# The second chunk's C product as seven block products, in a gated mix of a state-space layer and a dense layer

## The chip, the cores and the metric

The kernel runs on one core of a Trainium2 chip. The metric is the device time of one execution in microseconds, given as the median of the runs.

## What is computed

The input x has 2048 tokens of 640 features. Two branches are computed from it and mixed by a gate for each token:

```python
g = sigmoid((x * gate_w).sum(-1, keepdims=True))
h[t] = Lam_bar * h[t-1] + B_bar @ x[t]            # complex, 640 states
a = 2.0 * einsum("blp,dp->bld", h, Cmat).real + x * Dskip
b = gelu(x @ w1 + b1) @ w2 + b2                   # 640 -> 1728 -> 640
return g * a + (1 - g) * b
```

Data are bfloat16; the output is bfloat16.

## The kernel before, in words

**Tiling.** The tokens are cut into four chunks of 512 (CH). A chunk has four token tiles of 128; the first two are its first half, the last two its second. The 640 states are five rows of 128 (KS), the 640 output features two halves of 320 (HD).

**Stages of a chunk c.** `ff1(c)` multiplies x by w1 (65 + 20 matmuls), and ScalarE writes the gelu into `gel[c]`. `ssm(c)` multiplies x by B (50 matmuls): for each of the five rows ScalarE evicts two PSUM banks into a `bu` tile (eight of them, in turn). VectorE then works on the row (`scan_ops`): three products and sums turn it (`cos_in`, `sin_in`, `sum_in`, which frees `bu`), two scans along the tokens, three more turn it back (`cos_out`, `sin_out`, `sum_out`) into the state tile `hs[c]`. Rows are counted through all chunks: chunk 0 has rows 0 to 4, chunk 3 rows 15 to 19. `fin_b(c)` multiplies `gel[c]` by w2 and leaves (1-g)·b in float32 tiles `gbs`. Then the states are multiplied by C and combined with `gbs` into the output tile `ot`, which a DMA stores.

**Two forms of the C product.** `hs[c]` has four blocks of 128 x 5 x 256: a and b are the real and imaginary states of the chunk's first half, g21 and d those of the second half. C has four blocks as well: C11 and C12 are the two halves of `CT_re` by output feature, C21 and C22 those of `CT_im`.
- `fin_a(c)` (line 799) multiplies directly: 4 token tiles x 2 halves x 10 matmuls = 80 (line 812). The skip term x·D is put into the PSUM banks beforehand by ScalarE (`seed`, line 664, which also loads the x tile of the chunk after), and one VectorE instruction for each half of a tile makes the output (line 817). Chunks 0 and 1 use it.
- `fin_s(c)` (line 865) is a Strassen form in Winograd's ordering: seven block products instead of eight, 7 x 2 x 5 = 70 matmuls (line 877). It needs sums of blocks. From the states: M7 = a - g21, then g21 + d in g21's place, M6 = a - (g21 + d), M3 = b + M6 (`h_sums`, line 838, four VectorE instructions of 128x1280). From C: U7 = C12 - C22, U6 = U7 - C11, and U5 and U4, which are C22 and C21 plus U6. Partial sums X are forked by ScalarE into other banks (Y, Z, W), product 7 is added on VectorE (`part_7`, line 901), the skip term is added to `gbs` by VectorE (`skip_in`, line 855), and `done` (line 886) makes the output. Products run in the order 1, 7, 2, 6, 5, 3, 4, each for two token tiles. Chunks 2 and 3 use it. `fin_b` is of the same form.

**Sums made by transfers.** `plus(dst, src)` (line 676) is a DMA issued by POOL that adds src onto dst in SBUF; `minus(dst, src)` (line 681) is a ScalarE copy with scale -1. `minus_c(c)` and `minus_d(c)` make the sums that `fin_b(c)` needs, in the tiles N3 and N2, from `gel[c]`. U4 to U7 are made in this way during `ff1(3)`, out of two copies on SP, two negations on ScalarE and four additions.

**Order.** The order of instructions on each engine is that of the program (a manual schedule). For VectorE a small planner keeps clocks for TensorE, ScalarE and VectorE. The operations of scan rows wait in a list `pend`. `dve_now(ready, cost, fn)` first lets out of the list what would start, by VectorE's clock, ahead of `ready`, and then emits fn. `let_out(0, c)` lets out everything up to the last row of chunk c:

```python
def let_out(until, chunk=-1):
    while pend:
        ready, cost, fn, _ = pend[0]
        start = max(ck.dve, ready)
        if start >= until and not any(x[3] == chunk for x in pend if chunk >= 0):
            return
        pend.pop(0); fn(); ck.dve = start + cost
```

SP and POOL work through their transfers in program order too; a transfer that waits holds those behind it. TensorE's order around the change is ff1(2), fin_a(0), ssm(2), fin_b(1), fin_a(1), ssm(3), ff1(3), fin_b(2), fin_s(2), fin_b(3), fin_s(3).

**Names that the change touches.** `xA` and `xB` hold transposed x: chunks 0 and 3 in xA, 1 and 2 in xB. `load_xT(3)` (line 128) is issued ahead of ssm(2). `gates(c)` (line 644) makes columns of g and 1-g. `skips(c, a)` multiplies x tiles by D on VectorE. `gated(c)` (line 849) puts g·x·D of two token tiles into the tiles GS[c] on ScalarE. `settle` issues small ScalarE work for the scans' carries. The dictionaries given to a stage hold work to be issued at numbered places of it ("hooks").

Of the kernel before, what the change touches and what calls it, by code (L numbers as in the profile page):

```python
# [16 lines left out]
P = 128  # L17
# [25 lines left out]
def kernel(  # L43
# [40 lines left out]
    xA, xB = (const.tile([P, KD, CH], BF16, name=n) for n in ("xA", "xB"))  # L84
    xT = [xA, xB, xB, xA]
    w1a_sb = const.tile([P, KD, cut1], BF16, name="w1a_sb")
# [10 lines left out]
    CT_re = const.tile([P, KS, D], BF16, name="CT_re")  # L97
    CT_im = const.tile([P, KS, D], BF16, name="CT_im")
    TCOS = const.tile([P, KS, CH], BF16, name="TCOS")
    TSIN2 = const.tile([P, KS, 2, CH], BF16, name="TSIN2")  # L100
# [75 lines left out]
    HC = CH // 6 + 1  # L176
    tfi = work.tile([P, HC], I32, name="e", bufs=1)
    nc.gpsimd.iota(tfi[:], pattern=[[1, HC]], base=0, channel_multiplier=0)
    rows(nc.gpsimd, prmA[0:KS, :], A_log_dt)
# [6 lines left out]
    NP = NQ + HC  # L186
    tf = const.tile([P, NP], F32, name="tf")
    for i, m in enumerate((1.0, float(CH), float(CH // 2), float(2 * HC - 2))):
# [70 lines left out]
    nc.vector.memset(halfpi[:], HALF_PI)  # L259
    nc.vector.tensor_copy(out=tf[:, NQ:NP], in_=tfi[:])  # L260
    ones = lambda n: nc.const_aps.tensor(1.0, [P, n], BF16)
# [103 lines left out]

    scr = gelp.tile([P, KF * CH // 2], F32, name="gel")
    gel_tile(0)
# [19 lines left out]
    cq = col("cq", n=NQ * KS)  # L387
    kk = work.tile([P, KS, NP], I32, name="bu", bufs=8)
    sth, cth = sq[:, 0:KS], cq[:, 0:KS]
# [25 lines left out]
    nc.vector.tensor_tensor(out=thp_c[:], in0=dt16[:], in1=limp[:], op=ALU.mult)  # L415
    nc.vector.tensor_tensor(out=u, in0=tf[:].rearrange("p (o i) -> p o i", o=1).to_broadcast([P, KS, NP]), in1=over(thp_c[:], NP), op=ALU.mult)
    part(0, 2)
# [58 lines left out]
    def inputs(c, ks):  # L476
        bu = work.tile([P, 2, CH], BF16, name="bu", bufs=8)
        for ri, BT in enumerate((BT_re, BT_im)):
            p = bank()
            for kd in range(KD):  # L480
                nc.tensor.matmul(p[:], lhsT=BT[ks >= KSA][:, kd, (ks % KSA if ks < KSA else ks - KSA) * P:][:, 0:P], rhs=xT[c][:, kd, :],  # L481
                                 start=(kd == 0), stop=(kd == KD - 1))
                pe(CH)
            nc.scalar.activation(out=bu[:, ri, :], in_=p[:], func=ACT.Identity)  # L484
            act(0.6)
        return bu, ck.act
# [64 lines left out]
    def scan_ops(c, ks, bu, ready):  # L551
# [55 lines left out]
        def sum_out():  # L607
# [3 lines left out]

        new = [(ready, 0.61, cos_in, -1), (0, 0.61, sin_in, -1), (0, 0.61, sum_in, -1), (0, 1.23, lambda: scan(0), -1),
               (0, 1.21, lambda: scan(1), -1), (0, 0.3 if c == 0 else 0.1 if c < NCH - 1 else 0, ends if c < NCH - 1 else lambda: None, -1),
               (0, 0.61, cos_out, -1), (0, 0.61, sin_out, -1), (0, 0.63, sum_out, c)]
        old = latest.ops
# [28 lines left out]
    def gates(c):  # L644
        sl = slice(c * TPC, (c + 1) * TPC)

        def f():
            nc.vector.tensor_scalar(out=gcol[:, 0, sl], in0=gz[:, sl], scalar1=0.5, scalar2=0.5, op0=ALU.mult, op1=ALU.add)
            nc.vector.tensor_scalar(out=gcol[:, 1, sl], in0=gz[:, sl], scalar1=-0.5, scalar2=0.5, op0=ALU.mult, op1=ALU.add)
            nc.vector.tensor_scalar(out=gcol[:, 2, sl], in0=gz[:, sl], scalar1=0.5, scalar2=-0.5, op0=ALU.mult, op1=ALU.add)  # L650

        dve_now(ck.act + 0.3 if c > 0 else ck.pe, 0.2, f)
# [8 lines left out]
    def skip(ti):  # L661
        dve_now(ck.pe, 0.45, lambda: nc.vector.tensor_tensor(out=xn[ti][:], in0=xn[ti][:], in1=Dbc[:], op=ALU.mult))

# [57 lines left out]
    def fin_b(c, at={}, gs=None):  # L721
# [58 lines left out]
        both("X", N2, TB)  # L780
        fork("X", "Z")
        if c < NCH - 1:
            part_7()
# [45 lines left out]
    narrow = lambda t, n: t.rearrange("p k t -> p (k t)")[:, 0:n]  # L829
    U5, U7, U6, U4 = (narrow(t, KS * HD).rearrange("p (k d) -> p k d", k=KS) for t in (BT_re[1][:], BT_im[1][:], xB[:], w1b_sb[:]))  # L830
    M6, M7 = (t[:].rearrange("p k t -> p (k t)").rearrange("p (k t) -> p k t", k=KS) for t in (BT_im[0], BT_re[0]))
    M3 = narrow(xA[:], KS * HT).rearrange("p (k t) -> p k t", k=KS)
    C11, C12, C21, C22 = (t[:, :, h * HD:(h + 1) * HD] for t in (CT_re, CT_im) for h in range(2))

    def add(out, x, y, op):
        return lambda: nc.vector.tensor_tensor(out=flat(out), in0=flat(x), in1=flat(y), op=op)

    def h_sums(c):
        (a, b), (g21, d) = ([hs[c][:, i, r] for r in range(2)] for i in range(2))
        steps = []  # L840
        for out, x, y, op in ((M7, a, g21, ALU.subtract), (g21, g21, d, ALU.add), (M6, a, g21, ALU.subtract), (M3, b, M6, ALU.add)):
            steps.append(lambda fn=add(out, x, y, op): dve_now(0, 0.8, fn))
        return steps, (a, M7, M6, b, g21, M3, d), (C11, U7, U6, C21, U5, C22, U4)

    wide = [narrow(w1a_sb[:], 6 * D)[:, j * 2 * D:(j + 1) * 2 * D].bitcast(F32) for j in range(3)]
    wide += [xA[:].rearrange("p k t -> p (k t)")[:, KS * HT:].bitcast(F32), narrow(w1c_lo[:], 2 * D).bitcast(F32)]
    GS = {2: wide[0:2], 3: wide[3:5]}
# [7 lines left out]
    def skip_in(c, tiles, d0, d1, ready=0):  # L855
        for a in tiles:
            ti = c * TPC + a
            if a >= H:
                dve_now(ready, 0.82, lambda: nc.vector.tensor_tensor(out=gbs[ti][:], in0=gbs[ti][:], in1=GS[c][a - H], op=ALU.add))
                continue  # L860
            dve_now(ready, 0.88 if d1 - d0 > HD else 0.48, lambda: nc.vector.scalar_tensor_tensor(
                out=gbs[ti][:, d0:d1], in0=xn[ti][:, d0:d1], scalar=gcol[:, 0, ti:ti + 1],
                in1=gbs[ti][:, d0:d1], op0=ALU.mult, op1=ALU.add))

    def fin_s(c, lhs, rhs, at={}):
        A = dict(zip((1, 7, 6, 2, 5, 3, 4), lhs))
# [19 lines left out]
        def done(t, j, half, h, d0=0, d1=HD):  # L886
            ti = c * TPC + half * H + j
            first = ti not in ots
            if first:
                ots[ti] = fwork.tile([P, D], BF16, name="ot", bufs=4)  # L890
            o = h * HD
            dve_now(ck.pe + 0.2, 0.54, lambda: nc.vector.scalar_tensor_tensor(  # L892
                out=ots[ti][:, o + d0:o + d1], in0=t[j][:, d0:d1], scalar=gcol[:, 0, ti:ti + 1],
# [7 lines left out]
        def part_7(j):  # L901
            gb, ti = gbs[c * TPC + H + j], c * TPC + H + j
            wide = lambda t: t.rearrange("p (h d) -> p h d", h=2)
            dve_now(ck.act, 0.88, lambda: nc.vector.scalar_tensor_tensor(
                out=wide(gb[:]), in0=q[j][:].rearrange("p (o d) -> p o d", o=1).to_broadcast([P, 2, HD]),
                scalar=gcol[:, 3, ti:ti + 1], in1=wide(gb[:]), op0=ALU.mult, op1=ALU.add))
# [10 lines left out]
        for j in range(H):  # L917
            product(Q, 7, j, True)
            q[j] = fwork.tile([P, HD], F32, name="gq", bufs=2)
            nc.scalar.activation(out=q[j][:], in_=Q[j][:, 0:HD], func=ACT.Identity)  # L920
            act(0.44)
# [48 lines left out]
    def sums(c):  # L970
# [16 lines left out]
    gates(2)  # L987
    fin_a(0, sums(1))
    load_xT(3)
    ssm(2, {KS - 1: lambda: skips(1)})  # L990
    fin_b(1, seeds(1))
    fin_a(1, {**sums(2), 3: lambda: minus(U6, C22, 1.5)})
    ssm(3)
    gel_tile(3)
    nc.sync.dma_start(out=U7, in_=C12)
    steps, lhs, rhs = h_sums(2)
    ff1(3, 0, {1: lambda: (minus(U5, C11, 1.5), plus(U7, U6), plus(U5, C12), plus(U6, U5)),
               5: lambda: (skips(2), let_out(0, 2), [f() for f in steps[:3]]),
               7: lambda: (skips(2, H), [load_xn((NCH - 1) * TPC + H + j, narrow(w1a_sb[:], 6 * D)[:, (4 + j) * D:(5 + j) * D]) for j in range(H)]),
               10: lambda: (nc.sync.dma_start(out=U4, in_=C21), plus(U4, U6))})  # L1000
    for a, t in ((0, w1c_hi[:].rearrange("p k f -> p (k f)")[:, 0:D]), (1, xB[:].rearrange("p k t -> p (k t)")[:, KS * HD:KS * HD + D])):
        load_xn((NCH - 1) * TPC + a, t)
    gates(3)
    nc.vector.tensor_scalar(out=gcol[:, 3, NT - 2 * TPC:NT], in0=gcol[:, 0, NT - 2 * TPC:NT], scalar1=-1.0, scalar2=None, op0=ALU.mult)
    steps[3]()
    fin_b(2, {1: lambda: (gated(2), skips(3, H)),
              2: lambda: minus_c(3),
              3: lambda: (gated(3), skip_in(2, (0, 1), 0, HD))}, GS[2])
    last, lhs3, _ = h_sums(3)
    fin_s(2, lhs, rhs, {0: lambda: skip_in(2, (0, 1), HD, D, ck.act + 0.5), 1: lambda: (minus_d(3), skips(3))})  # L1010
    fin_b(3, {0: lambda: (let_out(1e9), [f() for f in last]),
              3: lambda: skip_in(3, (0, 1), 0, HD)}, GS[3])
    skip_in(3, (H, H + 1), 0, D)
    skip_in(3, (0, 1), HD, D)
    fin_s(3, lhs3, rhs)

# [29 lines left out]
```

## Time and profile before

| what | value |
|---|---|
| runs (3) | 206.68 to 207.22 us, median 206.85 |
| profiled execution | 206.56 us, its span 204.8 us |
| granted TensorE clock | 1.00 |
| fin_a(1) | 119.19 to 130.06 us, 80 matmuls |
| fin_s(2) | 168.80 to 178.41 us, 70 matmuls |
| VectorE busy in 119.19 to 130.06 | 10.87 us of 10.87 |
| VectorE busy in 168.80 to 178.41 | 7.58 us of 9.61 |
| ScalarE busy in 119.19 to 130.06 | 8.41 us |
| share of DMA time in 105.70 to 119.19 | 0.28 |

How to read the profile: all times count from the span's start. The page gives the busy time of each engine and, in 40 slices of the span, its busy share in tenths. The chain of waits is followed back from the last instruction; each of its rows is a start, a length and an engine with the tile that it writes and the line of the code. Groups and timelines name an instruction as out<-in with the shape, and in brackets the idle time ahead of it and what ended that. PE is TensorE, DVE VectorE, ACT ScalarE, POOL GpSimd and SP SyncE.

### The profile page before, as it was taken

The numbers are of one execution on the slowest core, as the hardware profiler recorded it, in microseconds if no ns is written. First come the engines' busy times: TensorE is split into PE (matmuls) and PEld (weight loads), VectorE is DVE, ScalarE is ACT, GpSimd is POOL, SyncE is SP. The second block draws the span as 40 slices with busy tenths as digits, with TensorE's granted clock in tenths as the row PEclk, the third lists the DMA queues.
The fourth block names the chain that finished last, engine by engine and source line by source line (L and its number), as shares of the span: only waits on it lengthen the run. The fifth ranks groups of instructions, "written<-read, shape, count | busy, mean of one in ns | idle before, by whom it ended". The sixth has DMA issues, their size and how long they took to land.

```text
span 204.8 us, 3592 instructions
## 1 busy us (share of the span) xinstructions
PE 200.6 (98%) x1301; PEld 119.3 (58%) x1301; DVE 186.6 (91%) x314; ACT 140.7 (69%) x271; POOL 50.6 (25%) x83
## 2 busy tenths in 40 slices
PE   8999999999999999999999999999999999999993
PEld 5744544454477544675457777544446777777762
DVE  2799999999999999999999999999999999686573
ACT  4696856997866799991764899266776699255520
POOL 8506930313330410031001052200412170124000
PEclk9999999999999999999999999999999999999999
DMA  6999999999999160159932369912596989719303
GB/s 192 193 144 223 194 303 158 203 224 287 177 210 219 23 109 15 50 104 239 194 90 53 74 120 234 235 35 80 89 190 121 182 159 198 175 24 208 60 0 128
DMA packets 45190, 30.28 MB, mean 148 GB/s; under 512 B 26898, under 2 KB 42612, under 8 KB 45172
## 3 DMA queue, kind: packets, MB, share of 16 engines
q0 software_dynamic: 6448, 12.53, 36.1%
q1 hardware_dynamic: 38148, 17.03, 35.5%
q10 hardware_dynamic: 576, 0.49, 0.7%
q8 instruction: 10, 0.16, 0.3%
q14 instruction: 8, 0.07, 0.1%
HBM read 7.79 MB, written 2.62 MB: 51 GB/s over the span
## 4 chain that ended last, share of the span: by engine, by line
PE 97%; DVE 1%; DVEq 0%; issue 0%
PE bank L305 28%; PE bank L732 26%; PE bank L481 21%; PE bank L812 11%; PE bank L877 9%; PE bank L264 1%; PE bank L329 1%; DVE ot L892 0%; PE bank L267 0%; DVE xA L274 0%; DVEq L1041 0%; PE bank L408 0%; PE bank L420 0%
## 5 line engine op out<-in xcount | busy, mean ns | idle before, releaser
L314 ACT ACTIVATE gel<-bank,colB 128x512 bf16<-128x512 f32 (+1 forms) x52 | 33.5, 692 | 7.9 <-PE bank L305 7.6
L575 DVE TENSOR_TENSOR_SCAN g<-r_c,carry,v 128x512 bf16<-128x512 f32 x30 | 38.3, 1277 | 0.0
L484 ACT ACTIVATE bu<-bank 128x512 bf16<-128x512 f32 x40 | 23.3, 600 | 19.3 <-PE bank L481 19.2
L732 PEld LDWEIGHTS <-gel 128*128 128x128 bf16 x280 | 27.3, 98 | 11.1 <-issue 0.2
L732 PE MATMUL bank<-w_sb,gel 128*128 128x320 bf16 x168 | 24.3, 299 | 0.0
L752 ACT ACTIVATE gb<-bank,gcol 128x320 f32<-128x320 f32 x32 | 16.2, 526 | 7.4 <-PE bank L732 6.9
L305 PEld LDWEIGHTS <-w1a_sb 128*128 128x128 bf16 x162 | 13.9, 98 | 12.0 <-issue 0.2
L812 PEld LDWEIGHTS <-hs 128*128 128x128 bf16 x160 | 15.6, 98 | 6.0
L481 PEld LDWEIGHTS <-BT_im 128*128 128x128 bf16 x100 | 9.7, 98 | 12.0 <-DMA BT_im<-in_A_B_im_dram 0.5
L481 PEld LDWEIGHTS <-BT_re 128*128 128x128 bf16 x100 | 9.6, 98 | 11.0
L744 ACT ACTIVATE bank<-bank 128x320 f32<-128x320 f32 x16 | 6.8, 423 | 11.0 <-PE bank L732 11.0
L305 PE MATMUL bank<-xA,w1a_sb 128*128 128x128 bf16 (+2 forms) x102 | 14.1, 291 | 0.0
L557 DVE TENSOR_TENSOR v<-wa,bu 128x1024 bf16<-128x1024 bf16 x20 | 13.7, 685 | 0.1
L557 DVE TENSOR_TENSOR hs<-wb,g 128x1024 bf16<-128x1024 bf16 x20 | 13.7, 685 | 0.1
L557 DVE TENSOR_TENSOR g<-TSIN,g 128x1024 bf16<-128x1024 bf16 x20 | 13.7, 685 | 0.1
L557 DVE TENSOR_TENSOR wb<-TCOS,g 128x1024 bf16<-128x1024 bf16 x20 | 13.7, 686 | 0.0
L557 DVE TENSOR_TENSOR bu<-TSIN,bu 128x1024 bf16<-128x1024 bf16 x20 | 13.6, 682 | 0.1
L812 PE MATMUL bank<-CT_re,hs 128*128 128x320 bf16 x80 | 13.5, 299 | 0.0
L812 PE MATMUL bank<-CT_im,hs 128*128 128x320 bf16 x80 | 13.5, 299 | 0.0
L732 PEld LDWEIGHTS <-N 128*128 128x128 bf16 x112 | 11.0, 98 | 4.3
L557 DVE TENSOR_TENSOR wa<-TCOS,bu 128x1024 bf16<-128x1024 bf16 x20 | 13.4, 670 | 0.0
L305 PEld LDWEIGHTS <-w1b_sb 128*128 128x128 bf16 x80 | 7.7, 98 | 9.6 <-DMA w1b_sb<-in_B_w_dram 0.7
(193 smaller groups left out, 398.1 us busy)
## 6 DMA issues: line engine op xcount, KB each, us to landing
out_dram<-ot SPq DMA_DIRECT2D x15, 160.0 KB, 5.0
w_sb<-in_B_w_dram SPq DMA_DIRECT2D x4, 480.0 KB, 5.7
gel<-N POOLq DMA_DIRECT2D x4, 448.0 KB, 4.9
N<-gel POOLq DMA_DIRECT2D x3, 448.0 KB, 5.6
gel<-gel POOLq DMA_DIRECT2D x3, 448.0 KB, 7.3
N<-N POOLq DMA_DIRECT2D x3, 448.0 KB, 5.2
gb<-gq POOLq DMA_DIRECT2D x4, 320.0 KB, 4.8
xn<-in_A_x_dram SPq DMA_DIRECT2D x8, 160.0 KB, 4.2
```

The lines of the kernel that those rows point to most:

```text
L264: nc.tensor.matmul(pA[:, 0:n], lhsT=ones(P), rhs=ones(n), start=True, stop=True)
L305: nc.tensor.matmul(p[:, t0:t1], lhsT=w, rhs=xT[c][:, kd, t0:t1], start=(kd == 0) if first is None else first, stop=(kd == last), skip_grou ...
L314: nc.scalar.activation(out=dst, in_=src, func=ACT.Gelu_apprx_tanh, bias=b1_c[p0:p1, kf:kf + 1])
L481: nc.tensor.matmul(p[:], lhsT=BT[ks >= KSA][:, kd, (ks % KSA if ks < KSA else ks - KSA) * P:][:, 0:P], rhs=xT[c][:, kd, :], start=(kd == 0 ...
L484: nc.scalar.activation(out=bu[:, ri, :], in_=p[:], func=ACT.Identity)
L557: nc.vector.tensor_tensor(out=o, in0=a, in1=b, op=op)
L575: nc.vector.tensor_tensor_scan(s["g"][:, ri, :], r_c[:, ks:ks + 1].to_broadcast([P, CH]), s["v"][:, ri, :], init, ALU.mult, ALU.add)
L732: nc.tensor.matmul(p[:, 0:HD], lhsT=lhs[:, s, j * P:(j + 1) * P], rhs=rhs[:, s, :], start=fresh and s == 0, stop=s == KH - 1, skip_group_c ...
L744: nc.scalar.activation(out=quad[j][dst][:, 0:HD], in_=quad[j][src][:, 0:HD], func=ACT.Identity)
L752: nc.scalar.activation(out=gbs[ti][:, h * HD:(h + 1) * HD], in_=quad[j][name][:, 0:HD], func=ACT.Identity, scale=gcol[:, 1, ti:ti + 1])
L812: nc.tensor.matmul(p[:, 0:d1 - d0], lhsT=hs[c][:, a // H, j // KS, j % KS, (a % H) * P:][:, 0:P], rhs=CT[:, j % KS, d0:d1], start=False, s ...
L877: nc.tensor.matmul(t[j][:, d0:d1], lhsT=A[i][:, k, j * P:(j + 1) * P], rhs=B[i][:, k, d0:d1], start=fresh and k == 0, stop=k == KS - 1, sk ...
```

## The change

The second chunk takes `fin_s(1)` in place of `fin_a(1)`. That moves these things:
- U7 and U6 are made by VectorE right behind fin_a(0), U7 in the place of C12 (`sums_76`). U5 and U4 are C22 and C21, copied by SP, plus U6, added by POOL: once for chunk 1, in N3 and in a block of `gel[1]`, and once for chunks 2 and 3, in BT_re and BT_im during ff1(3).
- M7, g21 + d and M6 of chunks 1 and 2 are made by ScalarE negations and POOL additions (`sum_7`, `sum_6`); M3 stays on VectorE. Chunk 3 keeps `h_sums` on VectorE. M6 and M7 are tiles of their own.
- xT[3] is xB, so load_xT(3) stands behind ssm(2). minus_c(2) and minus_d(2) stand in ssm(3). The x tiles of chunk 2 are loaded behind fin_s(1).
- `bu` has six tiles instead of eight, and two small tables (tf, tfi) lie in a scratch tile.
- Chunk 1 gets no seeds; its skip terms come by `skip_in` on VectorE, and its copies of product 7 lie in `gel[1]`.
- gates(c > 0) makes the fourth column; gates(3) stands at hook 2 of fin_b(2). `fin_b` has a new hook 4 ahead of its third product into X.
- The planner's costs change: a turn 0.6 for 0.61, a scan 1.2 for 1.23 and 1.21, `skip` 0.4 for 0.45, `done` 0.47 for 0.54.

```diff
-    xT = [xA, xB, xB, xA]
+    xT = [xA, xB, xB, xB]
...
+    M6, M7 = (const.tile([P, KS, HT], BF16, name=n) for n in ("M6", "M7"))
...
-        bu = work.tile([P, 2, CH], BF16, name="bu", bufs=8)
+        bu = work.tile([P, 2, CH], BF16, name="bu", bufs=6)
...
+            if c > 0:
+                nc.vector.tensor_scalar(out=gcol[:, 3, sl], in0=gz[:, sl], scalar1=-0.5, scalar2=-0.5, op0=ALU.mult, op1=ALU.add)
...
         fork("X", "Z")
+        hook(4)
...
+    U7, U6 = C12, block(xA)
+    def U54(c):
+        return (block(N3), block(gel[1][:, 0, 0:KH, :])) if c == 1 else (block(BT_re[1]), block(BT_im[1]))
+    def M3(c):
+        return narrow((N2 if c == 1 else xB)[:], KS * HT).rearrange("p (k t) -> p k t", k=KS)
...
+    def sum_7(c):
+        let_out(0, c)
+        (a, _), (g21, d) = state(c)
+        minus(M7[:], g21, 1.25)
+        plus(flat(M7[:]), flat(a))
+        plus(flat(g21), flat(d))
+    def sum_6(c):
+        (a, _), (g21, _) = state(c)
+        minus(M6[:], g21, 1.25)
+        plus(flat(M6[:]), flat(a))
+    def sums_76():
+        for out, x, y in ((U7, C12, C22), (U6, U7, C11)):
+            dve_now(ck.pe + 0.3, 0.95, lambda: nc.vector.tensor_tensor(out=out, in0=x, in1=y, op=ALU.subtract))
+    def copy(dst, src):
+        nc.sync.dma_start(out=dst, in_=src)
...
     fin_a(0, sums(1))
+    sums_76()
+    ssm(2, {2: lambda: sum_7(1), KS - 1: lambda: (skips(1), skips(1, H))})
     load_xT(3)
-    ssm(2, {KS - 1: lambda: skips(1)})
-    fin_b(1, seeds(1))
-    fin_a(1, {**sums(2), 3: lambda: minus(U6, C22, 1.5)})
-    ssm(3)
+    U5, U4 = U54(1)
+    fin_b(1, {1: lambda: (sum_6(1), copy(U4, C21)),
+              4: lambda: (copy(U5, C22), plus(U4, U6), plus(U5, U6)),
+              3: lambda: skip_in(1, (0, 1), 0, HD)})
+    fin_s(1, {0: lambda: skip_in(1, (0, 1), HD, D, ck.act + 0.5), 1: h_sums(1)[3]})
+    for a in range(TPC):
+        load_xn(2 * TPC + a)
+    ssm(3, {1: lambda: minus_c(2), 3: lambda: minus_d(2)})
     gel_tile(3)
...
+    def load_early():
+        skips(2, H)
+        sum_7(2)
...
+    ff1(3, 0, {1: next_54, 5: lambda: (skips(2), let_out(0, 2)), 7: load_early})
...
+    fin_b(2, {1: lambda: (gated(2), sum_6(2), skips(3, H)),
+              2: lambda: (gates(3), minus_c(3)),
+              3: lambda: (gated(3), skip_in(2, (0, 1), 0, HD))}, GS[2])
+    fin_s(2, {0: lambda: (skip_in(2, (0, 1), HD, D, ck.act + 0.5), h_sums(2)[3]()), 1: lambda: (minus_d(3), skips(3))})
+    fin_b(3, {0: lambda: (let_out(1e9), [f() for f in h_sums(3)]),
+              3: lambda: skip_in(3, (0, 1), 0, HD)}, GS[3])
```

Here `next_54` copies C22 and C21 into U5 and U4 of chunk 2 and adds U6 to each, and `load_early` ends with the loads of two x tiles of chunk 3, as before.

## Prediction

> **What bounds the kernel now.** I read the page's busy shares first, then the chain of waits in order of time, then the groups and the timelines of the stages that the change touches.
>
> ```profile
> PE 200.6 (98%) x1301; PEld 119.3 (58%) x1301; DVE 186.6 (91%) x314; ACT 140.7 (69%) x271; POOL 50.6 (25%) x83
> ...
> PE   8999999999999999999999999999999999999993
> ...
> DVE  2799999999999999999999999999999999686573
> ```
>
> TensorE is busy in every slice but the last. VectorE is too until about 173 us (slices of 5.12 us); after that it has gaps.
>
> ```profile
> 107.62 11.57 PE bank L732 x84
> 119.19 10.87 PE bank L812 x80
> 130.06 10.79 PE bank L481 x50
> ...
> 155.49 13.31 PE bank L732 x98
> 168.80 9.61 PE bank L877 x70
> 178.41 13.31 PE bank L732 x98
> 191.72 9.02 PE bank L877 x65
> ```
>
> These are rows of the chain: start, length, what. One TensorE stage follows the other without a wait. The second chunk's C product is the row at 119.19; the same product of the third chunk, already in seven block products, is the row at 168.80. So what TensorE saves is saved in the end, if nothing that it waits for comes late. All chunks have the same sizes, so the row at 168.80 is a price for the new one.
>
> **TensorE.** 80 matmuls in 10.87 us go, 70 in 9.61 us come: **-1.26 us**. The weight loads fall with them. The granted clock is 1.00 in both stages. This is the only term on the path; everything else is cover, and I go through it by engine.
>
> **VectorE, 94 to 131 us.** Added, by start-to-start distances. U7 and U6: two subtractions of 128x1600. The nearest rows are 128x1280 at 0.73 alone and 0.86 behind its input (157.14 to 157.87, 146.95 to 147.81) and 128x1792 at 1.12 (41.22 to 42.34); I take 0.95 each, 1.9 in all, between 1.5 and 2.2. M3 of the second chunk: 0.73. Four skip additions of 128x320: 0.45 each (two in 0.90 at 167.04), 1.8. Two of 128x640 and two of part 7: 0.8 each, since a 128x640 row lasts 0.88; 3.2. The fourth gate column: 0.07 three times, less 0.08 for the instruction that it replaces. The eight results cost the same 0.46 each as in the old form. Sum: +7.7 us.
> Removed: the third chunk's M7, g21 and M6.
>
> ```profile
> 146.95 0.82 DVE L836 TENSOR_TENSOR BT_re<-hs 128x1280 bf16<-128x1280 bf16 x1
> 147.81 0.82 DVE L836 TENSOR_TENSOR hs<-hs 128x1280 bf16<-128x1280 bf16 x1
> 148.74 0.82 DVE L836 TENSOR_TENSOR BT_im<-hs 128x1280 bf16<-128x1280 bf16 x1
> 149.48 0.89 DVE L662 TENSOR_TENSOR xn<-xn,Dbc 128x640 bf16<-128x640 bf16 x2
> ```
>
> They hold VectorE from 146.95 to 149.48: -2.5 us. Net +5.2 us; TensorE being 1.26 earlier, VectorE is **6.5 us later against TensorE** than now. Who waits? The scan rows (six products and two scans a row, 6.2 us) have no reader on TensorE until fin_s(3), at 191.72. Results of fin_s go ahead of rows that are late, since the planner lets a row out only when its clock is not yet at the result's ready time. So the debt slides behind row 19 to fin_b(3). Now the last row ends at 172.0 and h_sums(3) gives M7 at 184.4, for a product that starts at 191.72 + 1.37 = 193.1: 8.7 us of room. And VectorE has idle time to repay from:
>
> ```profile
> 176.41 1.23 DVE L892 SCALAR_TENSOR_TENSOR ot<-bank,gcol,gb 128x320 bf16<-128x320 f32 x2 [1.76 <-PE bank L877]
> ...
> 181.19 0.89 DVE L904 SCALAR_TENSOR_TENSOR gb<-gq,gcol,gb 128x640 f32<-128x640 f32 x1 [0.46 <-ACT bank L744]
> ...
> 189.81 0.82 DVE L859 TENSOR_TENSOR gb<-gb,xA 128x640 f32<-128x640 f32 x1 [1.93 <-DMA xA<-gq]
> 191.76 0.83 DVE L859 TENSOR_TENSOR gb<-gb,w1c_lo 128x640 f32<-128x640 f32 x1 [1.12 <-DMA w1c_lo<-gq]
> ```
>
> The brackets are idle time and what ended it. With 0.76 and 0.69 at 193.5 and 195.15 they make 6.7 us, against a debt of 6.5: just enough, if the order on VectorE lets them be used. If none before 184 is, M7 comes at 190.9 and is still in time; the skip additions behind it are what is late. I take 0 on the path, up to +0.3 at the end.
>
> **The earlier uses of late VectorE work.** (a) sum_7(1): ScalarE's negation for M7 sits between the evictions of ssm(2) and waits for row 9. That row ends at 98.7 now; U7 and U6 go ahead of its last three operations, so 100.6, while ScalarE gets there at 99.8. Behind it are the evictions of ssm(2), each 0.60 in 1.08, so a hold of 0.8 + 1.2 us is made up, and eight PSUM banks cover it. Cost 0. (b) sum_7(2) needs row 14, which ends at 136.7 now and some 9 us later against TensorE before the three removed sums repay: 145.8, for a negation at about 148.5. Cost 0, with 2.7 us to spare and banks behind that. (c) The input buffers go from eight to six. A row then needs the buffer of the row six before it. Row 14 is evicted at 104, and row 8's was read by 82.9; row 19 at 140, and row 13's by 119.6, some 8 us later after the change. Cost 0.
>
> **ScalarE.** It loses eight seeds (0.39 each, 3.1 us) and gains eight copies in fin_s (0.42 each, 3.4), two negations of 128x1280 in the second chunk and two in the third. 128x1792 lasts 1.68 and 128x1600 1.52, so about 1.2 each; two of 1.52 go. The tight place is fin_b(2): gated(2) ends at 161.3 and the next copy starts at 162.24, released by TensorE. The M6 negation of 1.2 between them ends at 162.4: the copy is 0.1 late, and TensorE, which comes back to that bank at 163.1, sees nothing. Cost 0, with at most 0.2 allowed.
>
> **SP, POOL and the transfers.** load_xT(3) moves behind ssm(2), since its tile is now the one that ssm(2) reads: SP issues it at 105.7 instead of 96.95, and holds SP 4.1 to 5.7 us (the two like it). Its reader starts at 128.8, so it is early by far; but queued behind it on SP are the copies of C21 and C22 for U4 and U5. U5 also waits for the product that reads N3 (to 111.4). Then: copies issued by about 112.5, landing 3.2 later (the copy of the same size now), 115.7; the addition of U6 onto U5 is the second of two on POOL.
>
> ```profile
> gel<-N POOLq DMA_DIRECT2D x1, 448.0 KB, 5.9
> xn<-in_A_x_dram SPq DMA_DIRECT2D x4, 96.0 KB, 4.3
> ...
> BT_im<-xB POOLq DMA_DIRECT2D x1, 400.0 KB, 4.2
> BT_re<-CT_re POOLq DMA_DIRECT2D x1, 400.0 KB, 7.4
> ```
>
> Columns: size and us from issue to landing. Two additions of this size sent together took 4.2 and 7.4. Issued at about 115.5, U5 is ready between 119.7 and 123; its product starts at 119.19 + 8 x 0.686 = 124.7. Room: 1.7 to 5 us. U4 is needed at 127.4. M6 (issued at 111.5, on hs) is needed at 123.3, M7 and g21 (issued at 102 to 104, landing by 110) at 120.6 and for the M6 negation at 110.3. The first row above is b += N2 of the first chunk, beside the very transposes that now fall beside its twin of the second chunk, and took 5.9 for 7.3 of room. Cost 0, between 0 and 1.5.
>
> On that place the Trainium skill speaks against the change. SBUF - State Buffer, section "SBUF: two separate sides", says that a transfer sent from GpSimd can stand still because VectorE, in its two-port modes, keeps GpSimd from writing descriptors. The change adds six such transfers beside a full VectorE. The trace does not show the hold: b += N2 at 109.98, under a VectorE busy without a break, took 0.86 us to issue and 4.6 to land, where its kind took 4.5 to 5.9. By that page an addition could come one VectorE instruction late, at most a scan (1.28 us), still inside U5's room; by the trace, none does. The sum is the same by both.
>
> **The rest.** Scratch tiles at the start change place only; the rows near them show no wait, so 0, with +-0.1. minus_c(2) and minus_d(2) move into ssm(3), where ScalarE is busy 6.2 of 10.8 us; their products are over 20 us away. The third and fourth chunks' seven products read U7 in C's own place: same shapes, same price.
>
> **Sum.** The profiled execution took 206.56 us (span 204.8, 1.76 around it). 204.8 - 1.26 gives a span of 203.5 and 205.3 us. The median of the runs shown, 206.85, lies 0.29 above that execution; from it the same term gives **205.6 us**. What a measurement here can tell from no change is about 0.3%, 0.62 us.
>
> **Rivals.**
> *A, the forecast*: TensorE's 1.26 comes through, less up to 0.4: 205.1 (0.2 below the lowest of the runs less 1.26, with the terms below nothing) to 206.1. For it: every reader has room. Chance 0.64.
> *B, U5 late*: the transposes hold SP 5.7 us, the copies land at 117, the second addition takes its 7.4 beside the gb additions, and product 5 waits 0.5 to 1.6 us. 206.1 to 207.2. For it: the smallest room in the sum. Against it: DMA is at 0.28 of its time there. Chance 0.17.
> *C, VectorE's debt is not repaid* (the slower side): in fin_b(3) and fin_s(3). It decides once the debt against TensorE exceeds the 6.7 us of gaps, for instance because results are planned ahead of rows and the gaps of 176 and 181 stay empty while 2 us of waits for M3 and the gb additions are new. Debt 8.5 less the 4.5 after 184 leaves some 4; the last stage has 1.1 of its own idle time: +2.9 - 1.26, so 208.5 (207.5 to 209.5). For it: VectorE at 10.87 of 10.87 us in the stage that grows most. Against it: fin_s(2) kept TensorE running with the same list. Chance 0.12.
> *D, a hold on ScalarE* (gates(3), now at hook 2 behind late rows, before gated(3), before the last evictions and forks): fork Y late by up to 1 us, 205.9 to 207.5. Chance 0.07.
> The change doing other than it says is not a case of its own: the seven products are counted in the code.
>
> **Chances and range.** Faster by over 0.3% (below 206.23): all of A and a quarter of B and D, 0.70. Within 0.3%: the rest of B and D, 0.18. Slower: C, 0.12. The range from 205.1 to 207.2 leaves out C and little more.
>
> **What would show it.** Right: 70 matmuls of fin_s at 119.2 in 9.6 us, no waits on PE, ssm(3) at 128.8. B: a wait before the fifth product, released by a DMA onto U5. C: h_sums(3) after 191, and a last stage longer than 9.02 us ended by DVE. D: a wait at the product Y of fin_s(2). The sum would be wrong if the seven-product stage lost its pace, or if VectorE did not get through its list of 9.4 us in fin_s(1) soon enough to give PSUM banks to ssm(3).

## The result and the profile after

| | before | after |
|---|---|---|
| median of the runs | 206.93 us | 206.35 us |
| lowest | 206.50 us | 205.89 us |
| profiled execution (span) | 206.56 us (204.8) | 206.34 us (204.6) |

The ratio is 0.995, with a 95% interval from 0.9926 to 0.9973. The forecast was 205.6 us; the change brings 0.6 to 1.0 us of the 1.26 that were forecast. In some executions the granted clock was lower and the time longer; the ratios leave these out, medians and ranges hold all executions, and the one profiled execution of this kind, that of "M3 first, skips late" (212.48 us at a clock of 0.984), is not read.

From the page of the changed kernel, the busy shares and two of the lines of slices:

```profile
PE 198.8 (97%) x1280; PEld 118.6 (58%) x1291; DVE 191.5 (94%) x324; ACT 142.1 (69%) x273; POOL 54.8 (27%) x89
...
PE   8999999999999799999999999999999999999993
...
DVE  2699999999999999999999999999999999999873
```

TensorE is 1.8 us less busy than before, but the span is only 0.2 shorter: so TensorE waits, and one slice (the 14th, 66 to 72 us) says 7. VectorE is full until about 189 us, 15 us longer than before. The chain of that execution (start, length, what):

```profile
61.16 7.55 DMA gel<-N
68.71 0.05 issue
68.76 2.08 PE bank L735 x14
...
107.13 13.31 PE bank L735 x98
120.44 9.51 PE bank L911 x70
...
155.38 13.31 PE bank L735 x98
168.69 9.61 PE bank L911 x70
178.30 13.31 PE bank L735 x98
191.61 9.02 PE bank L911 x65
```

The new stage is there: 70 matmuls in 9.51 us where 80 took 10.87. But the chain goes through a transfer at 61 us, in fin_b(0), 35 us ahead of anything that the change edits for the second chunk. TensorE's list of waits names it, together with the only other one, at the start of the program:

```profile
PE bank L735 <- DMA gel<-N: 1.1, 1, 1.1
PE bank L266 <- PEq L1075: 0.8, 1, 0.8
```

(Columns: us in total, times, longest.) It is b += N2 of the first chunk, the addition that POOL issues and that the last product of fin_b(0) reads. In before's profiled execution it had landed in time. So my first reading was that the change cost a wait there. The experiments say otherwise.

A table of where the stages start, read from TensorE's timeline, carries most of what follows. All lengths in us; "start" is the start of ssm(1), "rest" the time from the start of fin_s(3) to the end of the execution.

| profiled execution | start | to ff1(2) | to fin_a/fin_s(1) | that stage | to fin_b(2) | fin_b(2) | fin_s(2) | fin_b(3) | rest | time |
|---|---|---|---|---|---|---|---|---|---|---|
| before | 45.13 | 24.11 | 49.79 | 10.87 | 25.43 | 13.31 | 9.61 | 13.31 | 15.00 | 206.56 |
| after | 45.34 | **25.33** | 49.61 | 9.50 | 25.43 | 13.32 | 9.61 | 13.31 | 14.89 | 206.34 |
| after, second run | 46.17 | **26.84** | 49.61 | 9.51 | 25.43 | 13.31 | 9.61 | 13.31 | 14.89 | 208.68 |
| after, third run | 45.41 | 24.11 | 49.60 | 9.51 | 25.43 | 13.31 | **10.74** | 13.31 | 14.88 | 206.30 |

The last row settles the form of the question. There the transfer landed in time, and the whole 1.1 us was lost all the same, 100 us later, in fin_s(2).

### The profile page after: what moved, and what is told of

The parts are those of the page before. It is cut to its first block, busy times and chain, and to the rows that moved or that the text cites. A ratio compares the mean times of both kernels' runs of the same rounds, so it can differ in the third digit from the quotient of the medians.

```text
span 204.6 us, 3594 instructions
## 1 busy us (share of the span) xinstructions
PE 198.8 (97%) x1280; PEld 118.6 (58%) x1291; DVE 191.5 (94%) x324; ACT 142.1 (69%) x273; POOL 54.8 (27%) x89
## 4 chain that ended last, share of the span: by engine, by line
PE 88%; DMA 8%; ACT 1%; issue 1%; DVE 0%; POOL 0%; DVEq 0%; SPq 0%; ACTq 0%; POOLq 0%
PE bank L307 28%; PE bank L735 21%; PE bank L482 18%; PE bank L911 14%; PE bank L816 5%; DMA gel<-N 4%; DMA gel<-gelN 3%; DMA gel<-eL 2%; PE bank L266 1%; PE bank L331 1%; DVE ot L926 0%; ACT xA L528 0%; PE bank L269 0%; POOL TC L680 0%; ACT bu L485 0%
## 5 line engine op out<-in xcount | busy, mean ns | idle before, releaser
L307 PE MATMUL bank<-xB,w1a_sb 128*128 128x512 bf16 x88 | 19.8, 379 | 0.1
L482 PE MATMUL bank<-xB,BT_im 128*128 128x512 bf16 x75 | 18.6, 379 | 0.0
L482 PE MATMUL bank<-xB,BT_re 128*128 128x512 bf16 x72 | 18.5, 379 | 0.2
L911 PEld LDWEIGHTS <-hs 128*128 128x128 bf16 x125 | 12.0, 98 | 4.5
L926 DVE SCALAR_TENSOR_TENSOR ot<-bank,gcol,gb 128x320 bf16<-128x320 f32 (+2 forms) x25 | 12.5, 532 | 1.9 <-PE bank L911 1.2
L307 PE MATMUL bank<-xB,w1b_sb 128*128 128x512 bf16 x59 | 13.4, 379 | 0.1
```

The costliest lines, as they stand in the source:

```text
L307: nc.tensor.matmul(p[:, t0:t1], lhsT=w, rhs=xT[c][:, kd, t0:t1], start=(kd == 0) if first is None else first, stop=(kd == last), skip_grou ...
L911: nc.tensor.matmul(t[j][:, d0:d1], lhsT=A[i][:, k, j * P:(j + 1) * P], rhs=B[i][:, k, d0:d1], start=fresh and k == 0, stop=k == KS - 1, sk ...
L926: dve_now(ck.pe + 0.2, 0.47, lambda: nc.vector.scalar_tensor_tensor(out=ots[ti][:, o + d0:o + d1], in0=t[j][:, d0:d1], scalar=gcol[:, 0, t ...
```

## The experiments

### The same two kernels again

> The changed kernel once more, unchanged. Its profiled execution lost 1.4 us ahead of 71 us, most of it in a wait of TensorE in fin_b(0) for the addition b += N2, and gained 1.6 us behind. Theory (chance): that wait is an accident of the crowded transfers before 65 us and no part of the change; SP and POOL have the same instructions in the same order up to 85 us in both kernels. Then this execution has fin_b(0) between 13.3 and 15 us, perhaps without a wait, and the time against before is 0.993 to 0.997. Rival (part of the change): the wait is there again at 1.0 to 1.5 us.

Measured: 206.58 us median (lowest 205.94), ratio 0.997 [0.9934, 1.0005]. Its profiled execution, 208.68, is the row "second run": two waits in fin_b(0) (for b += N2 and for a sum of weights), which make that stage 2.7 us longer. That is more than either expectation had.

> The kernel before once more, unchanged; a ratio of 1 within its interval. Theory (chance): its fin_b(0) can have the wait too, and the spans of its executions spread by 0.5 us or more. Rival (part of the change): fin_b(0) is 13.3 us again, without a wait. In both, fin_a(1) takes 10.87 us.

Measured: 207.45 us, ratio 1.0009 [0.9982, 1.0036]. No wait in fin_b(0); the execution is 0.9 us longer than before's only because ssm(1) starts at 46.01 and not at 45.13. That start differs from one execution to the next in both programs (45.13 to 46.17 in the profiles here), and is the better part of what the times of the profiled executions without a wait differ by.

### The early edits alone

```diff
+    M6, M7 = (const.tile([P, KS, HT], BF16, name=n)[:] for n in ("M6", "M7"))
...
-    tfi = work.tile([P, HC], I32, name="e", bufs=1)
+    tfi = scr[:, 5 * KS * P:5 * KS * P + HC].bitcast(I32)
...
-        bu = work.tile([P, 2, CH], BF16, name="bu", bufs=8)
+        bu = work.tile([P, 2, CH], BF16, name="bu", bufs=6)
```

The kernel before, with the scratch tiles, the six input buffers and the planner's costs of the change.

> The kernel before with those parts of the change that can act before 85 us, and no other: six bu tiles, the small tables in the scratch tile, M6 and M7 as tiles of their own, the planner's new costs. Rival (part of the change): these parts bring the wait in fin_b(0); slower than before by 0.5 to 1.4 us, with a wait of about 1 us for b += N2. Theory (chance): the same as before within 0.3 us.

Measured: 207.38 us, ratio 1.0009 [0.9979, 1.0039]; no wait in fin_b(0). Within that interval these edits cost nothing, as forecast.

### b += N2 of the first chunk on VectorE

```diff
-        plus(flat(b), flat(N2[:]))
+        if c == 0:
+            dve_now(ck.pe + 0.3, 1.0, lambda: nc.vector.tensor_tensor(out=flat(b), in0=flat(b), in1=flat(N2[:]), op=ALU.add))
+        else:
+            plus(flat(b), flat(N2[:]))
```

> The changed kernel with b += N2 of the first chunk made by VectorE (128x1792, about 1.1 us) instead of a transfer, so that TensorE cannot wait for that transfer. In both theories fin_b(0) is 13.3 us. Theory (chance): the median gains what the wait costs on average, 0.2 to 0.8 us against the changed kernel (0.990 to 0.995 against before). Rival (part of the change): it gains the whole 1.1 us (0.988 to 0.992). VectorE's 1.1 us more are not seen, since M7 of the last chunk has 6 us of room.

Measured: 207.49 us, ratio 0.9997 [0.9969, 1.0026]. The wait in fin_b(0) is gone (13.31 us), and nothing is gained, against both expectations: one more microsecond on VectorE, at 60 us, shows up on TensorE at 108 us. From TensorE's waits, and from ScalarE's timeline (start, length, what; in brackets the idle time ahead and what ended it):

```profile
PE bank L735 <- ACT bank L747: 1.1, 1, 1.1
```

```profile
103.68 1.27 ACT L685 ACTIVATE M<-hs 128x1280 bf16<-128x1280 bf16 x1 [3.31 <-DVE hs L558]
104.86 1.07 ACT L485 ACTIVATE bu<-bank 128x512 bf16<-128x512 f32 x2
```

This is use (a) of the prediction: the negation for M7 of the second chunk stands among ScalarE's evictions of ssm(2) and waits for row 9. In the changed kernel it waits 1.19 us (third run) and that is made up, as forecast (0.8); with 3.31 us the evictions and the first fork of fin_b(1) are late and TensorE stands for 1.05 us. So VectorE has no slack between 60 and 103 us: work that was added at one end was late at the other.

### The loads of x earlier, in both programs

```diff
+    load_skip()
     ssm(1, {2: lambda: fold(0), 4: lambda: fold(1)})
     gates(1)
     load_xT(2)
-    load_skip()
```

> The changed kernel with the loads of D and of the rest of the first x tiles (544 KB) issued ahead of ssm(1), at about 53 us, instead of behind load_xT(2), at 60 us, so that they no longer run beside b += N2. In both profiles of the changed kernel TensorE waited 1.2 and 2.7 us in fin_b(0) for the additions there, in none of those with the old tail. Theory (typical wait): most executions of the changed kernel wait about 1 us there, which is why its median is 0.6 us below before while its last 134 us are 1.54 us shorter; then this kernel has no wait in fin_b(0) and is 1.2 to 1.6 us below before (0.992 to 0.994). Rival (accident): those two executions were exceptions; 0.996 to 0.998, as the changed kernel.

Measured: 206.61 us, ratio 0.997 [0.995, 0.999]. The wait in fin_b(0) is still there, 1.0 us. The edit did not clear the place, so it does not test the theory: the loads went out at 55.0 to 58.8 us, but the transpose of x (load_xT(2)) behind them on SP moved from 56.4 to 58.9 us (third run and this one) and now lies beside b += N2, issued at 61.1.

> The kernel before with the same move of the loads. Where the wait in fin_b(0) belongs to the changed kernel, this one is the same as before within 0.2 us. Where it strikes both alike, it gains as much as r5 does against the changed kernel, 0.5 to 1 us.

Measured: ratio 1.0042 [1.0011, 1.0073], the times widely scattered (206.91 to 218.69 us): slower, which neither case of the expectation had. In TensorE's waits:

```profile
PE bank L732 <- DMA gel<-N: 1.0, 1, 1.0
```

That is before's program with the loads moved and none of the change in it, and it has the same wait (the three profiles of before's form without that move have none). What goes with the wait is how long the transfer took, in these lists of DMA issues from 55 to 66 us (size, us from issue to landing): the third run of the changed kernel, without the wait, and then this kernel.

```profile
gel<-N POOLq DMA_DIRECT2D x1, 448.0 KB, 6.1
...
xB<-in_A_x_dram SPq DMA_TRANSPOSE x1, 7.4
```

```profile
gel<-N POOLq DMA_DIRECT2D x1, 448.0 KB, 8.3
...
xB<-in_A_x_dram SPq DMA_TRANSPOSE x1, 11.0
```

Where it took 5.7 to 6.1 us TensorE does not wait; where it took 7.0 to 8.3, it does.

### More debt for VectorE

```diff
     def load_early():
         skips(2, H)
-        sum_7(2)
+        let_out(0, 2)
+        [f() for f in h_sums(2)[:3]]
...
-    fin_b(2, {1: lambda: (gated(2), sum_6(2), skips(3, H)),
+    fin_b(2, {1: lambda: (gated(2), skips(3, H)),
```

The third chunk's M7, g21 and M6 back on VectorE, which is 2.5 us more for it.

> The changed kernel with the third chunk's M7, g21 + d and M6 made by VectorE as before (three times 0.86 us in ff1(3)) instead of two negations and three transfers: VectorE's debt is 2.5 us larger from there on. If VectorE has the room of 5 to 6 us that the prediction gave it, no change; TensorE's stages keep their length. If there is little room (b += N2 on VectorE at 62 us cost a wait of 1.1 in fin_b(1) and 0.5 in fin_s(2)), M3 of the third chunk comes late in fin_s(2): a wait of 1 to 2.5 us there, slower than the changed kernel by that.

Measured: 207.29 us, ratio 0.9981 [0.9951, 1.001]. fin_b(0) does not wait (13.31), yet:

```profile
PE bank L911 <- DVE xB L844: 0.9, 1, 0.9
PE bank L911 <- DVE ot L926: 0.8, 1, 0.8
```

The first wait is in fin_s(2), which takes 10.62 us; `xB` is M3 of the third chunk. The second is in the last stage, which is 0.8 longer: TensorE waits there until VectorE has read a bank for a result. The expectation put the cost in the first wait; but the changed kernel without this edit (next section) has that wait at the same length (0.90), so the added 2.5 us show only at the end. There the total of VectorE's work does count: this kernel is 1.0 us slower than the changed one (206.31). The wait for M3 was the first sign of where the change itself gives back its gain.

### The changed kernel a third time

> The changed kernel, unchanged, a third time, on the chip of the three others. Theory (typical wait): a wait of 0.8 to 2 us in fin_b(0) again, 0.997 of before. Rival (accident): none.

Measured: 206.31 us (205.90 to 207.11), ratio 0.9957 [0.9941, 0.9974]; the profiled execution is the row "third run" above. TensorE in fin_s(2):

```profile
172.97 1.52 PE L911 MATMUL bank<-BT_re,hs 128*128 128x320 bf16 x10
175.39 1.53 PE L911 MATMUL bank<-CT_im,xB 128*128 128x320 bf16 x10 [0.90 <-DVE xB L844]
176.75 1.52 PE L911 MATMUL bank<-BT_im,hs 128*128 128x320 bf16 x10
```

These are products 5, 3 and 4. Product 3 waits for `xB`, and here is VectorE:

```profile
168.50 0.98 DVE L893 SCALAR_TENSOR_TENSOR gb<-xn,gcol,gb 128x320 f32<-128x320 bf16 x2
169.40 0.68 DVE L558 TENSOR_TENSOR bu<-TSIN,bu 128x1024 bf16<-128x1024 bf16 x1
...
173.00 0.66 DVE L558 TENSOR_TENSOR hs<-wb,g 128x1024 bf16<-128x1024 bf16 x1
173.59 1.00 DVE L893 SCALAR_TENSOR_TENSOR gb<-xn,gcol,gb 128x320 f32<-128x320 bf16 x2
174.51 0.82 DVE L844 TENSOR_TENSOR xB<-hs,M 128x1280 bf16<-128x1280 bf16 x1
```

M3's last input, M6, is this addition on POOL, which took 3.8 us and so landed at about 165.3:

```profile
161.48 0.86 POOL L680 DMA_DIRECT2D M<-hs  x1 [2.30 <-ACT M L685]
```

M3 starts at 174.51 because six row operations, 169.40 to 173.59, and two skip additions stand ahead of it. None of them is needed by TensorE before product 3: the `skip_in` in front of M3 let the rows out, since they would start, by the planner's clock, ahead of ScalarE's time plus 0.5.

One formula fits the profiles with this order. Product 3 starts at the later of TensorE's own pace, 6.89 us behind the start of fin_s(2) (that is the distance where nothing waits), and the end of M3:

| | fin_s(2) starts | + 6.89 | M3 ends | product 3 starts |
|---|---|---|---|---|
| after, first run | 168.53 | 175.42 | 174.97 | 175.42 |
| after, third run | 167.37 | 174.26 | 175.33 | 175.39 |
| more debt | 167.90 | 174.79 | 175.73 | 175.79 |
| b += N2 on VectorE | 168.82 | 175.71 | 175.91 | 175.96 |
| debt taken away (below) | 167.92 | 174.81 | 175.50 | 175.55 |

(With the loads of x earlier, product 3 starts at 176.32, 0.23 behind its pace; M3 had ended at 175.42, and the delay is there already at product 5: the chain names ScalarE's fork into its bank, at 174.43, behind a copy that had waited for a transfer and behind a negation. In the third run 0.12 of the delay is there at product 5 too.)

So the wait in fin_b(0), as long as it is about 1.2 us or less, and the wait for M3 are one loss in two places. Where the transfer of fin_b(0) has already held TensorE up by 1.2 us, it comes to product 3 after M3 and pays nothing there; where not, it pays 1.1 for M3. That is why the first and the third profile, one with the wait in fin_b(0) and one without, take the same time, 206.34 and 206.30. In the second run fin_b(0) lost 2.7 us; the 1.6 beyond this are paid, and its 208.68 us are 2.4 above the third run, 0.8 of it by the later start.

What was still open: is it M3's place in VectorE's order, or the sum of VectorE's work, which would come out somewhere else if M3 went ahead? The last four kernels were made for that.

### M3 first

```diff
-    fin_s(2, {0: lambda: (skip_in(2, (0, 1), HD, D, ck.act + 0.5), h_sums(2)[3]()), ...
+    fin_s(2, {0: lambda: (h_sums(2)[3](), skip_in(2, (0, 1), HD, D, ck.act + 0.5)), ...
```

> In the changed kernel M3 of the third chunk stands at VectorE's place 174.51 (execution without a wait in fin_b(0)), behind 4.2 us of row operations and 0.9 us of skip additions that skip_in lets out first, and product 3 waits 0.90 us for it; its input M6 had landed by about 165.3. Here M3 is put in front of skip_in at the same place of the program. Theory (place of M3 in VectorE's order): M3 starts at about 169.4, no wait for xB on TensorE, fin_s(2) 9.6 to 9.9 us in place of 10.7, and where fin_b(0) does not wait, the execution is 0.7 to 1.1 us shorter: 205.2 to 205.7, ratio to before 0.991 to 0.993. Rival (VectorE's total debt, not one place): the first result of product 2 stays at about 176.05, the banks of fin_b(3) wait for it, 0.8 to 1.0 us come back as waits for ot or for a bank, fin_s(2) plus fin_b(3) stays at 24.0 or more (13.31 + 10.7), 206.2 to 206.6, ratio 0.996.

Measured: 205.95 us (205.35 to 206.68), ratio 0.9945 [0.9929, 0.9962]. VectorE and then TensorE in fin_s(2):

```profile
168.97 0.98 DVE L893 SCALAR_TENSOR_TENSOR gb<-xn,gcol,gb 128x320 f32<-128x320 bf16 x2
169.87 0.81 DVE L844 TENSOR_TENSOR xB<-hs,M 128x1280 bf16<-128x1280 bf16 x1
170.61 0.68 DVE L558 TENSOR_TENSOR bu<-TSIN,bu 128x1024 bf16<-128x1024 bf16 x1
```

```profile
174.18 1.52 PE L911 MATMUL bank<-BT_re,hs 128*128 128x320 bf16 x10
175.59 1.52 PE L911 MATMUL bank<-CT_im,xB 128*128 128x320 bf16 x10
```

M3 ends at 170.7, five microseconds ahead of product 3. That execution does not prove it by its length: its start was late (46.09) and the stretch of fin_b(0) was 0.64 longer (a wait for b += N2 again), so at 175.59 even the old place of M3 would have held. The times point the same way: the lowest is 1.08 us below before's lowest taken alongside, where the changed kernel's lowest was 0.65 below (205.90 against 206.55). They are no proof, since the interval of this ratio overlaps with those of the changed kernel (0.995 and 0.9957). The median is above the bound of the theory by 0.25, and below the rival's by as much.

### Debt taken away

```diff
-    ssm(2, {2: lambda: sum_7(1), KS - 1: lambda: (skips(1), skips(1, H))})
+    ssm(2, {2: lambda: sum_7(1)})
```

> Leaves out the multiplication of the second chunk's four x tiles by D (four VectorE instructions of 128x640, 0.40 us each from start to start, 1.6 in all, near 116 us), so the second chunk's skip term lacks D. Everything later on VectorE comes 1.6 us earlier as long as it is saturated; nothing else changes. Theory (VectorE, saturated from 45 to 186 us, sets M3 of the third chunk): M3 at about 172.9, product 3 does not wait, fin_s(2) 9.6 to 9.8, execution 205.2 to 205.6, ratio 0.991 to 0.993. Rival (the lost microsecond is not VectorE's: the transfer wait in fin_b(0), or TensorE's own pace): 206.2 to 206.6, ratio 0.996, as the changed kernel.

Measured: 206.77 us, ratio 0.9978 [0.9951, 1.0006]. My own expectation failed: with 1.6 us of VectorE's work gone at 105 us, nothing was gained. M3 is no earlier:

```profile
171.84 1.27 DVE L576 TENSOR_TENSOR_SCAN g<-r_c,carry,v 128x512 bf16<-128x512 f32 x1
173.14 0.69 DVE L558 TENSOR_TENSOR wb<-TCOS,g 128x1024 bf16<-128x1024 bf16 x1
173.75 1.01 DVE L893 SCALAR_TENSOR_TENSOR gb<-xn,gcol,gb 128x320 f32<-128x320 bf16 x2
174.68 0.82 DVE L844 TENSOR_TENSOR xB<-hs,M 128x1280 bf16<-128x1280 bf16 x1
...
190.07 0.83 DVE L891 TENSOR_TENSOR gb<-gb,xB 128x640 f32<-128x640 f32 x1 [0.59 <-DMA xB<-gq]
191.71 0.82 DVE L891 TENSOR_TENSOR gb<-gb,w1c_lo 128x640 f32<-128x640 f32 x1 [0.81 <-DMA w1c_lo<-gq]
```

The planner let two more row operations (the scan and the product in the first two rows) out ahead of `skip_in`, and M3 stands at 174.68 where it stood at 174.51; product 3 waits 0.63 us. M3 of the second chunk was late in the same way (125.57 for 124.94), with a wait of 0.2 us; with it TensorE is 0.55 late at the start of fin_s(2). The 1.6 us come back as idle time behind 189 us, where nobody needs them. That speaks against the total as the cause of this wait: less work, M3 in the same place behind what `skip_in` lets out, and a wait again. It also corrects my theory, which had M3 move with the total.

### M3 earlier still

```diff
-              3: lambda: (gated(3), skip_in(2, (0, 1), 0, HD))}, GS[2])
+              3: lambda: (gated(3), h_sums(2)[3](), skip_in(2, (0, 1), 0, HD))}, GS[2])
```

and M3 taken out of hook 0 of fin_s(2).

> M3 of the third chunk still earlier, at hook 3 of fin_b(2) ahead of its skip additions, about 168.5 on VectorE in place of 174.5. Theory (M3's place): as with M3 first in fin_s(2), no wait for xB, fin_s(2) 9.6 to 9.9, 205.2 to 205.7. Risk that both theories share: gated(3), the evictions and the skip additions of fin_b(2) are then 0.8 us later on VectorE, which no TensorE work reads before the results. Rival (total debt): a wait for a bank behind ot in its place, 206.2 to 206.6.

Measured: 206.09 us (lowest 205.62), ratio 0.9967 [0.9943, 0.9992]. The stage fin_s(2) takes 9.61, without a wait for M3, which VectorE makes here:

```profile
168.45 0.79 DVE L844 TENSOR_TENSOR xB<-hs,M 128x1280 bf16<-128x1280 bf16 x1
```

The median lies between the two forecasts and meets neither. This is not better than M3 first; the profiled execution again had a wait in fin_b(0) (0.54 us). With M3 in a better place such a wait no longer hides anything, and it may be what the medians of these two kernels lack; that is argued, not shown.

### M3 first, skips late

```diff
-    fin_s(2, {0: lambda: (skip_in(2, (0, 1), HD, D, ck.act + 0.5), h_sums(2)[3]()), 1: lambda: (minus_d(3), skips(3))})
-    fin_b(3, {0: lambda: (let_out(1e9), [f() for f in h_sums(3)]),
+    fin_s(2, {0: lambda: (h_sums(2)[3](), skip_in(2, (0, 1), HD, D, ck.act + 0.5)), 1: lambda: minus_d(3)})
+    fin_b(3, {0: lambda: (let_out(1e9), [f() for f in h_sums(3)], skips(3)),
```

> M3 first in fin_s(2), and the two multiplications of chunk 4's first x tiles by D (0.8 us on VectorE at 175.25, ahead of the first results of product 2) moved behind the last rows in fin_b(3). Theory (place of M3, then the place of the results that free PSUM banks for fin_b(3)): the first result comes 0.8 us earlier than with M3 first alone; if that run still shows a wait for a bank, it is gone here: fin_s(2) 9.6, fin_b(3) 13.3, 205.1 to 205.5. Rival (total debt): the 0.8 us only go behind the last rows, fin_s(3)'s first sums or the gb additions come 0.8 us later, and the last stage is longer than 9.02 by as much: 206 to 206.5.

Measured: 205.46 us, lowest 204.91, ratio 0.9926 [0.9902, 0.9949]. It beats before by 1.5 us (the ratio; its interval is 1.1 to 2.0), and by 1.52 in the lowest times. Of the 41 executions of the changed kernel none took less than 205.89 us; of this one 8 of 10 did, with M3 first alone 3 of 12, with M3 earlier still 1 of 12. By these counts the two moves together recover most of the loss, and M3's place alone showed 0.2 to 0.4 us of it in the medians (205.95 and 206.09 for 206.35). Adding the shortest lengths of the changed kernel's stages in the table to its third run's start gives 45.41 + 24.11 + 49.60 + 9.50 + 25.43 + 13.31 + 9.61 + 13.31 + 14.88 = 205.16, an estimate for an execution without a wait; the median is 0.3 above it. What the 0.5 us against M3 first alone are is not shown by any profile, and the two intervals overlap. The expectation was that the first results of product 2, which free PSUM banks and stand behind the two `skips(3)`, come 0.8 us earlier.

## Why the prediction was right, and where it was wrong

Sign and range held. The size did not: 205.6 was forecast, 206.35 measured. That the range held is in part luck: the time lies above rival A's 205.1 to 206.1, the forecast, and inside the range because that was stretched to 207.2 for rival B, which did not come; what did come was none of the rivals.

- **TensorE's term, -1.26.** Right, and a little small: the stage went from 10.87 to 9.51, 0.1 below the twin of the third chunk that served as its price. Two terms that were not forecast go the same way: the stretch ahead of it is 0.19 shorter (49.79 to 49.60, in the first product of fin_b(1)), and the rest behind fin_s(3) 0.12. Together 1.67 us. Less the 1.13 of the next point that is 0.54, against 0.58 between the medians; and 1.5 (1.1 to 2.0) arrive in "M3 first, skips late".
- **The step that failed** is that the scan rows "have no reader on TensorE until fin_s(3)", and with it the list of "earlier uses of late VectorE work", (a) to (c). For the rows of the last chunk it is true. But M3 of the third chunk stands on the same engine behind those rows, and product 3 of fin_s(2) reads it. The kernel before made it at 157.14, 18 us ahead of its use at 175.53 (VectorE, then TensorE, in before):

```profile
157.14 0.81 DVE L836 TENSOR_TENSOR xA<-hs,BT_im 128x1280 bf16<-128x1280 bf16 x1
```

```profile
175.53 1.52 PE L877 MATMUL bank<-CT_im,xA 128*128 128x320 bf16 x10
```

  The change moves it to hook 0 of fin_s(2), behind a `skip_in` that lets rows out. The diff showed the line; I counted the third chunk's M3 as work that stays and did not ask what is queued ahead of it in its new place. Price: 1.13 us in fin_s(2) (third run), or about nothing there where fin_b(0) has already lost as much.
- **"I take 0 on the path, up to +0.3 at the end"** for the debt. The end was right: VectorE's busy time grew by 4.9 us where a net 5.2 was forecast, and the debt was repaid by the end of fin_b(3), as VectorE's timeline of the first profile shows:

```profile
185.82 0.69 DVE L558 TENSOR_TENSOR hs<-wb,g 128x1024 bf16<-128x1024 bf16 x1
186.54 0.83 DVE L844 TENSOR_TENSOR M<-hs 128x1280 bf16<-128x1280 bf16 x1
...
194.16 0.89 DVE L938 SCALAR_TENSOR_TENSOR gb<-gq,gcol,gb 128x640 f32<-128x640 f32 x1 [0.71 <-ACT gq L954]
```

  M7 is done at 187.4, between the 184.4 of before and the 190.9 of the worst case, and VectorE has idle time again at 194. The room was small: with 2.5 us more ("More debt for VectorE") the last stage is 0.8 longer. Rival C (not repaid, 208.5) did not come. It had named "waits for M3" as a possible cost of the last chunk, but not on TensorE.
- **U7 and U6** at 0.95 each: 97.47 to 99.40 in the third run, 0.97 each. Use (a), a hold of 0.8 on ScalarE that is made up: 1.19, made up. Its room is smaller than I thought: one more microsecond breaks it (b += N2 on VectorE).
- **U5**, the smallest room of the sum: 1.7 to 5 us forecast. In the first profile POOL issued it at 118.21 and it landed at 124.4, for a product at 125.7: room 1.3 us, below the range; in the third run it landed at 124.1 for a product at 124.56, room 0.4. load_xT(3) held SP for 2.71 us, less than the 4.1 to 5.7 taken; the copies landed later than thought, and the addition took 6.2. The argument against B, a DMA share of 0.28 at that place, was a number of the kernel before: in the changed one the same view of fin_b(1) gives 0.96 (first run) and 1.04 (third). No wait; rival B did not come, but by little.
- **GpSimd's transfers beside a full VectorE.** The Trainium skill, SBUF - State Buffer, section "SBUF: two separate sides", warns that VectorE can keep GpSimd from writing descriptors. It speaks of VectorE's two-port modes, and no run here shows which of these instructions run in one. In the changed kernel the additions between 100 and 124 us took 0.86 us to issue where nothing stood ahead of them, as before, and landed 5.5 to 6.3 us after it in the third run (up to 8.0 in the first); TensorE waited for none. No run here shows the hold; why they took longer to land than the 4.5 to 5.9 that I had cited from before is not shown either.
- **ScalarE in fin_b(2)**, 0.1 late: the fork stands at 162.24 right behind the negation (161.08 + 1.26 with its overlap), and TensorE did not wait there. Rival D did not come; its upper bound, 207.5, does not follow from its own "up to 1 us", which gives 206.6.
- **The transfer b += N2 in fin_b(0)** was cited as having 7.3 us of room for 5.9. It took 7.0 to 8.2 in five of eight profiles of the changed program and its variants, and 8.3 in one of four of before's form (the one with the loads of x earlier). Without that move it is four of seven against none of three. SP's instructions and POOL's transfers up to there are the same in both programs. Whether the change makes it more frequent can't be told from so few, and is left open; in the changed kernel a wait of 1.1 there costs nothing on top, in one with M3 in a better place it should.

## What to carry to other kernels

When work is moved onto an engine that is already full, list every instruction of that engine that another engine reads, and for each the place in the queue and what stands ahead of it; the reader's room counts from that, not from when the inputs are ready. The planner here, which fills with background work, gave no slack back when work was removed: it filled again, and the late instruction was as late; moving it to the front ended its wait. And when a wait is found in one profile of a changed kernel, look at a second profile before building on it: here the wait that the chain showed first was only hiding the one that mattered.

## What the runs showed that was not expected

- The same addition of 448 KB from SBUF onto SBUF, at the same place of the program, took 5.7 to 8.3 us from issue to landing in different executions. Where it was slow, the transpose beside it was mostly slow too (6.9 and 8.3 to 11.0, for 6.7 to 8.4 where it was fast).
- The time from the first instruction to ssm(1) varies by 1.0 us (45.13 to 46.17) among these executions, in both programs. A single profiled execution therefore says little about a change of 0.3%; the lengths of stages in it say much, since without a wait they repeat within 0.06 us.
